# Linear attention feeding a tanh-shrink MLP: the kv product of batch 1 set between its transposes, the numerator beside the denominator, and batch 2's phi moved

## The chip, the cores and the metric

The kernel runs on one core of a Trainium2 chip. The metric is the device time of one execution in microseconds; the median of several runs is compared. PE is the matrix engine (TensorE), PEld its weight loads, DVE the vector engine, ACT the scalar engine, POOL GpSimd, and SP the engine whose queue issues most transfers.

## What is computed

q, k and v have 8 batches, 8 heads, 576 tokens and 64 features. Cut to what matters:

```python
def phi(x):
    return np.where(x > 0, x, np.exp(x) - 1.0) + 1.0
q_p, k_p = phi(q), phi(k)
kv  = einsum('bhsd,bhse->bhde', k_p, v)
z   = sum(k_p, axis=2)
num = einsum('bhsd,bhde->bhse', q_p, kv)
den = einsum('bhsd,bhd->bhs', q_p, z)[..., None] + 1e-06
x   = (num / den), heads joined: 4608 tokens x 512
h   = x @ w_in                  # 512 -> 2048
out = (h - tanh(h)) @ w_out     # 2048 -> 512
```

## The kernel before

**Two streams of work on one PE.** The MLP is cut into nine chunks of 512 tokens (the loop over `c`, with `NC = 9`). In each chunk the first layer (L366) has 16 steps `fi`, of four 128x512 matmuls each, and the second layer (L387) has 16 steps `s`, also of four. Between the steps the attention of a later batch is slipped in: the lists `s1[fi]` and `s2[s]` hold functions that are called after the matmuls of that step. In chunk `c` the attention of batch `n1 = c + 1` is finished, and phi of batch `n2 = c + 2` is computed. The order is written out by hand (`tc.manual_schedule()`): what the program says first stands first in its engine's queue, and only waits on semaphores are put in.

**PSUM banks.** There are eight. In chunk 0 the layer-1 steps go through all of them, and its layer 2 accumulates four output tiles in banks 0 to 3 at the same time: there `g = s // 4` is the group of four `fi` and `i = s % 4` the tile, so that steps 8 to 11 need the third quarter of `w_out` and steps 12 to 15 the last one. Attention work of chunk 0 goes through banks 4 to 7 in turn (`side`). From chunk 1 on the MLP uses banks 0 to 5 in turn (`dense`) and the attention banks 6 and 7 (`attn`).

**One batch of attention.** `phi_pieces` gives three instructions for half `i` of a batch: an exp on ACT (`e`, L134), max and add on DVE (`r`, L135) and a min on DVE (`y`, L136). qp is then transposed into `qT`, by PE and two copies (`a_qT_pe`: L164, copied out by ACT at L168 and by DVE at L170) for batch 1, and by a transposing transfer from SP's queue (`a_qT_dma`, L153) from batch 2 on. `a_kv` (L177, batch 1) and `a_kv_cols` (L199, later batches, on a widened copy of v, `vp`, L189) compute kv and z; a DVE multiplication with a mask puts them into `kz` (L186, L202). `a_den` makes the denominators (16 small matmuls at L276, then L281 and the reciprocal at L285). For batch 1 `a_split` cuts the reciprocals into two bf16 parts (L295 to L298, result `w`), `num1` computes the numerators (four small matmuls L320, four large L317) and ACT copies them into `ns` (L346, L344), and `spread1` spreads `w` over the partitions by matmuls (L354, eight for two pairs, banks 4 to 7) and multiplies (L359) into `xT`, the input of layer 1. For later batches the reciprocals go through DRAM (`a_spread`: L305, L308, tile `rdb`) and `a_num` multiplies the numerators with them (L317, L328). `b0_scale_rest` (L320, L263) is the last piece of batch 0.

**Work around the change.** ACT copies finished output tiles out of PSUM (`evac`, L396, tile `osb`), and SP stores them (L401). In layer 1, ACT computes tanh of two banks (L372) and DVE subtracts (`gT`, L373), which frees the banks. POOL issues the loads of q, k and v; `gate` (L383) is a copy on POOL that waits for qT, and the loads of the next batch stand behind it. q and k have one buffer each, so a load also waits until phi has read the batch before.

Of the kernel before, what the change touches and what calls it, by code (L numbers as in the profile page):

```python
# [18 lines left out]
def kernel(  # L19
# [43 lines left out]
    attn = Banks([6, 7])  # L63
# [78 lines left out]
    def a_kphi(b, i):  # L142
        phi(b, k_t, kp_t, "kp", i)
# [13 lines left out]
    def a_qT_pe(b, i, banks, on=None):  # L157
        if i == 0:
            new_qT(b)
        for n in range(2):  # L160
            j0, j1 = ((0, 5), (5, 9))[n]
            ps = banks().bitcast(BF16).rearrange("p (j t) -> p j t", t=128)
            for j in range(j0, j1):
                nc.tensor.transpose(ps[:, j - j0, :], qp_t[b][:, i, j].rearrange("p h d -> p (h d)"), ident)  # L164
            src = ps[:, 0:j1 - j0, :]
            dst = qT_t[b][:, i, j0:j1].rearrange("p j g t -> p j (g t)")
            if (on or "AV")[n] == "A":
                nc.scalar.copy(dst, src)  # L168
            else:
                nc.vector.tensor_copy(dst, src)  # L170
# [9 lines left out]
    def a_kv(b, banks):  # L180
        kz_t[b] = kz_c[b % 2]
        ps = [banks()[:, 0:384].rearrange("p (i e) -> p i e", i=2) for hg in range(2)]
        for i in range(2):
            kv_mm(b, i, [ps[hg][:, i, :] for hg in range(2)])
        for hg in range(2):
            nc.vector.tensor_mul(kz_t[b][:, hg], ps[hg][:, :, 0:160], mask[:, hg])  # L186
# [80 lines left out]
    def a_den(b, banks, parts=range(4)):  # L267

        kz, qT = kz_t[b], qT_t[b]
        ps = banks()[:, 0:J * 16]  # L270
        for t in range(4) if b == 0 else ():
            nc.tensor.matmul(ps[32 * t:32 * t + 32], eps[:, 0:32], one[:, 0:J * 16], start=True, stop=False)
        for n, p in enumerate((0, 2, 1, 3)):
            if n in parts:
                for t in range(4):
                    nc.tensor.matmul(ps[32 * t:32 * t + 32], kz[:, p // 2, p % 2, 128:160],  # L276
                                     qT[:, p % 2, :, p // 2, 16 * t:16 * t + 16],
                                     start=(n == 0 and b > 0), stop=(n == NP - 1))
        if b > 0:
            den = rpool.tile([128, J * 16], F32, name="den")  # L280
            nc.vector.tensor_scalar(den, ps, 1e-6, None, ALU.add)  # L281
        else:
            den = ps
        rden = rpool.tile([128, J * 16], F32, name="rden")
        nc.vector.reciprocal(rden, den)  # L285
        rden_t[b] = rden

    def a_split(b):

        f = rden_t[b]  # L290
        t1 = rpool.tile([128, J * 16], BF16, name="t1")
        u = rpool.tile([128, J * 16], F32, name="u")
        t2 = rpool.tile([128, J * 16], BF16, name="t2")
        w = rpool.tile([128, J * 16], BF16, name="w")
        nc.vector.tensor_copy(t1, f)  # L295
        nc.vector.scalar_tensor_tensor(u, t1, part[:, 0:1], f, ALU.mult, ALU.add)
        nc.vector.tensor_copy(t2, u)
        nc.vector.scalar_tensor_tensor(w, t2, part[:, 1:2], u, ALU.mult, ALU.add)  # L298
        rden_t[b] = w
# [202 lines left out]
    for c in range(NC):  # L502
        gT = gpool.tile([128, NF, 512], BF16, name="gT")
        n1, n2 = c + 1, c + 2
        s1 = {i: [] for i in range(16)}
        s2 = {i: [] for i in range(16)}
        if c == 0:
            side = Banks([4, 5, 6, 7])
            sub = {}

            def spread1(h):
                sub["bp"] = a_spread_pe(1, 4, (2 * h, 2 * h + 1))
                for p in (2 * h, 2 * h + 1):
                    a_scale(1, p, sub["ns"], sub["bp"], 144 * (p % 2))

            def num1():
                sub["ns"] = new_ns(1)
                for p in (NP, 0, 1, 2, 3):
                    a_num_copy(1, sub["ns"], p, side)

            s1[11].append(lambda: a_kphi(1, 0))
            s1[13].append(lambda: a_kphi(1, 1))
            s2[3].append(lambda: a_qphi(1, 0))
            s2[4].append(lambda: (a_qphi(1, 1), load_q(2), load_k(2), load_v(2)))
            s2[0].append(prepare)
            s2[7].append(lambda: (a_qT_pe(1, 0, side), a_qT_pe(1, 1, side), a_kv(1, side)))
            s2[8].append(lambda: b0_scale_rest(side))
            s2[9].append(lambda: a_den(1, side))
            s2[10].append(lambda: (num1(), a_split(1)))
            s2[11].append(lambda: spread1(0))  # L530

            def q2(n):
                if n == 0:
                    sub["q"] = [phi_pieces(2, q_t, qp_t, "qp", i) for i in range(2)]
                if n < 2:
                    for f in sub["q"][n][:2]:
                        f()
                else:
                    for x in sub["q"]:
                        x[2]()  # L540
                    a_qT_dma(2)

            s2[12].append(lambda: q2(0))
            s2[13].append(lambda: (spread1(1), q2(1)))
            s2[14].append(lambda: q2(2))
            s2[15].append(lambda: a_kphi(2, 0))
        elif n1 < B:
            s1[7 if c == 1 else 5].append(lambda: a_kv_cols(n1, attn))
            s1[10 if c == 1 else 8].append(lambda: (a_den(n1, attn), a_spread(n1)))
            for p in range(NP + 1):  # L550
                s2[(11 if c == 1 else 9) + p].append(lambda p=p: a_num(n1, p))
        if c == 1:
            s1[1].append(lambda: a_kphi(2, 1))
            for i in range(2):
                s1[3].append(lambda i=i: a_vp(2, i))
        if c >= 1 and n2 < B:

            s1[0].append(lambda: (gate(qT_t[n1]), load_k(n2), load_q(n2), load_v(n2)))
            d = 2
            s2[d].append(lambda: a_kphi(n2, 0))  # L560
            s2[d + 2].append(lambda: a_kphi(n2, 1))
            s2[d + 4].append(lambda: a_qphi(n2, 0))
            s2[d + 6].append(lambda: (a_qphi(n2, 1), a_qT_dma(n2)))
            for i in range(2):
                s2[14 + i].append(lambda i=i: a_vp(n2, i))
        if c == 0:

            first = Banks([4, 5, 6, 7, 0, 1, 2, 3])
            hs = [ps_all[:, n, :] for n in range(4)]
            order = [((0, 0), (0, 1)), ((2, 0), (2, 1), (0, 2), (0, 3), (2, 2), (2, 3)),  # L570
                     [(p, fi) for p in (1, 3) for fi in range(4)]]
            seen = [0] * 4
            for n, part_ in enumerate(order):
                if n == 1:
                    open2()
                for p, fi in part_:
                    l1mm(c, fi, hs[fi], p, seen[fi])
                    seen[fi] += 1
            for fi in range(4):
                l1act(fi, hs[fi], gT)  # L580
        for fi in range(4 if c == 0 else 0, NF):
            h = first() if c == 0 else dense()
            for p in range(NP):
                l1mm(c, fi, h, p, p)
            if c == 0:
                l1act(fi, h, gT)
            elif fi % 2:
                n = dense.order[(dense.n - 1) % 6]
                l1act2(fi - 1, ps_all[:, n - 1:n + 1, :], gT)
            for f in s1[fi]:  # L590
                f()
        os_ = {}
        for s in range(16):

            (g, i) = divmod(s, 4) if c == 0 else (s % 4, s // 4)
            if g == 0:
                os_[i] = ps_all[:, i, :] if c == 0 else dense()
            if c == NC - 1 and i == 3:

                if g == 0:  # L600
                    o2 = dense()
                    for o, f in ((os_[i], slice(0, 384)), (o2, slice(384, DM))):
                        for fi in range(NF):
                            nc.tensor.matmul(o[:, f], gT[:, fi, 384:512], w_out_sb[:, fi, f],
                                             start=(fi == 0), stop=(fi == NF - 1))
                        evac(c, i, o, f.start, f.stop)
                continue
            l2mm(gT, os_[i], i, 4 * g, 4 * g + 4)
            if g == 3:
                evac(c, i, os_[i])  # L610
            for f in s2[s]:
                f()
# [30 lines left out]
```

## Time and profile before

| what | value |
|---|---|
| median of 8 runs | 294.84 us (294.64 to 295.11) |
| the profiled execution's own time | 294.67 us |
| its span | 292.9 us |
| PE busy | 283.5 us, 97% of the span, 1772 instructions |
| DVE busy | 174.8 us, 60% |
| ACT busy | 139.6 us, 48% |
| granted TensorE clock | 0.999 |
| transfers | 38.94 MB in 39077 packets |

The span is that of the recorded instructions; the time of an execution is 1.8 us longer. Busy shares are means over the whole span. Chunk 0 with its layer 2 lies at about 17 to 51 us, chunk 1 at 51 to 82 us; after that a chunk takes about 30 us.

### The profile page before, as it was taken

The page shows a single profiled execution, that of the slowest core. Times are in us where ns is not written, and L with a number is a line of the kernel's source. Part 1 is how long each engine was busy: PE and PEld are TensorE (multiplying, and loading weights), DVE is VectorE, ACT ScalarE, POOL GpSimd, SP SyncE. Part 2 cuts the span into 40 slices and gives each one's busy share as a digit, 9 for nine tenths or more (in the row PEclk, how much of TensorE's full clock was granted, in tenths as well). Part 3 has the DMA queues.
Part 4 walks back from the last instruction along what each step waited for, and adds up shares of the span by engine and source line. Part 5 has one row for each costly group of instructions (what it writes and reads, how often), then busy time and mean ns, then how long its engine had stood idle before and what let it go on. Part 6 is the DMA issues. An engine that isn't in the chain of part 4 may idle for free.

```text
span 292.9 us, 4475 instructions
## 1 busy us (share of the span) xinstructions
PE 283.5 (97%) x1772; PEld 134.3 (46%) x1801; DVE 174.8 (60%) x265; ACT 139.6 (48%) x168; POOL 33.6 (11%) x55
## 2 busy tenths in 40 slices
PE   8999998999999999999999999999999999999994
PEld 2544453454444444544454445444444444444443
DVE  4759857887557764786478646865581457106600
ACT  4938537947344643465246524661552155126411
POOL 8673030030030003000300020000000000000000
PEclk9999999999999999999999999999999999999999
DMA  6999999998989658955895569666117310130032
GB/s 101 195 202 213 207 207 218 204 146 153 241 157 179 161 120 136 215 131 121 137 222 128 133 135 189 138 147 140 38 28 174 73 36 0 39 83 23 0 74 72
DMA packets 39077, 38.94 MB, mean 133 GB/s; under 512 B 16336, under 2 KB 33808, under 8 KB 38288
## 3 DMA queue, kind: packets, MB, share of 16 engines
q0 software_dynamic: 17552, 18.35, 38.6%
q1 hardware_dynamic: 21344, 20.17, 30.2%
q8 instruction: 14, 0.23, 0.3%
q10 hardware_dynamic: 160, 0.13, 0.1%
q14 instruction: 7, 0.06, 0.1%
HBM read 43.91 MB, written 9.55 MB: 183 GB/s over the span
## 4 chain that ended last, share of the span: by engine, by line
PE 75%; DMA 13%; issue 7%; POOL 2%; ACT 1%; DVE 0%; SPq 0%; POOLq 0%
PE ps_all L366 36%; PE ps_all L387 34%; DMA qraw<-in_q_dram 5%; DMA w_in_sb<-in_moe_w_in_dram 3%; PE ps_all L199 2%; DMA out_dram<-osb 2%; DMA kraw<-in_k_dram 2%; PE ps_all L317 2%; PE ps_all L276 1%; ACT osb L396 1%; SPq L401 0%; POOL qraw L90 0%; ACT e L134 0%; POOL kraw L93 0%; DVE qp L136 0%
## 5 line engine op out<-in xcount | busy, mean ns | idle before, releaser
L366 PE MATMUL ps_all<-xT,w_in_sb 128*128 128x512 bf16 x560 | 127.0, 379 | 1.1 <-DVE xT L244 0.3
L387 PE MATMUL ps_all<-w_out_sb,gT 128*128 128x512 bf16 x547 | 126.3, 379 | 0.7
L373 DVE TENSOR_TENSOR gT<-ps_all,th 128x1024 bf16<-128x1024 f32 x64 | 77.9, 1219 | 59.7 <-ACT th L372 59.7
L372 ACT ACTIVATE th<-ps_all 128x1024 f32<-128x1024 f32 x64 | 65.5, 1024 | 57.0 <-PE ps_all L366 46.4
L366 PEld LDWEIGHTS <-w_in_sb 128*128 128x128 bf16 x576 | 55.2, 98 | 66.6 <-issue 0.6
L387 PEld LDWEIGHTS <-gT 128*128 128x128 bf16 x560 | 54.1, 98 | 64.2 <-issue 0.2
L396 ACT COPY osb<-ps_all 128x512 f32<-128x512 f32 (+1 forms) x36 | 20.9, 583 | 73.4 <-PE ps_all L387 54.2
L328 DVE TENSOR_TENSOR xT<-ps_all,rdb 128x512 bf16<-128x512 f32 x24 | 16.4, 690 | 13.3 <-PE ps_all L317 11.2
L134 ACT ACTIVATE e<-qraw 128x1152 bf16<-128x1152 bf16 x16 | 18.5, 1162 | 6.9 <-DMA qraw<-in_q_dram 6.9
L134 ACT ACTIVATE e<-kraw 128x1152 bf16<-128x1152 bf16 x15 | 17.5, 1165 | 0.0
L136 DVE TENSOR_TENSOR qp<-e,r 128x1152 bf16<-128x1152 bf16 x16 | 12.0, 757 | 7.8 <-ACT e L134 7.2
L136 DVE TENSOR_TENSOR kp<-e,r 128x1152 bf16<-128x1152 bf16 x15 | 11.4, 758 | 8.1 <-ACT e L134 7.3
L383 POOL COPY g<-qT 1x1 bf16<-1x1 bf16 x5 | 1.4, 271 | 120.5 <-DMA qT<-qp 120.5
L378 DVE TENSOR_TENSOR gT<-ps_all,th 128x512 bf16<-128x512 f32 x16 | 10.3, 686 | 2.4 <-ACT th L377 1.7
L377 ACT ACTIVATE th<-ps_all 128x512 f32<-128x512 f32 x16 | 9.2, 598 | 4.3 <-PE ps_all L366 3.1
L317 PE MATMUL ps_all<-qT,kz 128*128 128x512 bf16 x28 | 10.1, 379 | 0.0
L444 PE MATMUL ps_all<-zero 128*128 128x512 bf16 x29 | 8.8, 463 | 1.2 <-DVE zero L405 1.2
L135 DVE TENSOR_SCALAR r<-qraw 128x1152 bf16<-128x1152 bf16 x16 | 7.3, 454 | 2.2 <-DMA qraw<-in_q_dram 2.2
L199 PE MATMUL ps_all<-vp,kp 64*128 64x136 bf16 x216 | 7.4, 220 | 0.4 <-POOL g L383 0.4
L199 PEld LDWEIGHTS <-kp 64*128 64x128 bf16 x216 | 6.4, 94 | 3.0 <-issue 2.1
L285 DVE RECIPROCAL rden<-den 128x144 f32<-128x144 f32 x7 | 7.4, 1053 | 0.2
L394 DVE COPY osb<-ps_all 128x128 f32<-128x128 f32 x1 | 0.3, 292 | 11.6 <-DMA out_dram<-osb 11.6
(82 smaller groups left out, 121.8 us busy)
## 6 DMA issues: line engine op xcount, KB each, us to landing
out_dram<-osb SPq DMA_DIRECT2D x70, 128.0 KB
rdb<-ds SPq DMA_DIRECT2D x12, 576.0 KB
kraw<-in_k_dram POOLq DMA_DIRECT2D x7, 576.0 KB, 7.1
qraw<-in_q_dram POOLq DMA_DIRECT2D x7, 576.0 KB, 9.3
v<-in_v_dram POOLq DMA_DIRECT2D x7, 576.0 KB, 11.7
w_out_sb<-in_moe_w_out_dram POOLq DMA_DIRECT2D x4, 512.0 KB, 16.1
w_in_sb<-in_moe_w_in_dram POOLq DMA_DIRECT2D x6, 256.0 KB, 9.0
qraw<-in_q_dram POOLq DMA_DIRECT2D x2, 288.0 KB, 4.5
```

Source lines behind the costliest of these rows:

```text
L134: return (lambda: nc.scalar.activation(e, x, AF.Exp), lambda: nc.vector.tensor_scalar(r, x, 0.0, 1.0, ALU.max, ALU.add), lambda: nc.vector ...
L136: lambda: nc.vector.tensor_tensor(y, e, r, ALU.min))
L199: nc.tensor.matmul(ps[hg][:, i, :], kp[r, i, j].rearrange("p h d -> p (h d)"), vp[r, i, j, :], start=(j == 0), stop=(j == J - 1))
L317: nc.tensor.matmul(ps, kz[:, p // 2, p % 2, 0:128], qT[:, p % 2, 0:8, p // 2, :], start=True, stop=True)
L328: nc.vector.tensor_mul(xT[:, p, S * b:S * b + 512].rearrange("p (j t c) -> p j t c", j=8, t=4), ps.rearrange("p j (t c) -> p j t c", t=4), ...
L366: nc.tensor.matmul(h, w_in_sb[:, 2 * (p % 2) + p // 2, fi * 128:(fi + 1) * 128], xT[:, p, c * 512:(c + 1) * 512], start=(n == 0), stop=(n ...
L372: nc.scalar.activation(th, h, AF.Tanh)
L373: nc.vector.tensor_sub(gT[:, fi:fi + 2, :], h, th)
L377: nc.scalar.activation(th, h, AF.Tanh)
L378: nc.vector.tensor_sub(gT[:, fi, :], h, th)
L387: nc.tensor.matmul(o, gT[:, fi, i * 128:(i + 1) * 128], w_out_sb[:, fi, :], start=(fi == 0), stop=(fi == NF - 1))
L396: nc.scalar.copy(osb[:, f0:f1], o[:, f0:f1])
```

## The change

It touches chunk 0's layer 2 and the start of chunk 1.

1. At step 7, `a_kv(1)` is called between the two halves of `a_qT_pe(1, ...)`, not behind both. The banks are handed out in that order, so the products go to banks 6 and 7, and the second half's transposes to 4 and 5 again.
2. `num1` and `a_split(1)` are called right behind `a_den(1)` at step 9, not at step 10: `num1` passes the four matmuls of step 10. The first spread stays behind step 11.
3. phi of batch 2: the exp of q's first half and its two DVE instructions move from step 12 to step 11, behind the first spread; on ACT this exp now stands ahead of the copy of the first output tile. The exp of the second half moves from step 13 to step 12 and that of k's first half from step 15 to step 13. On DVE the first min now stands ahead of the second spread's multiplications. SP's transposing transfer of batch 2's q moves from step 14 to step 13; in SP's queue it stood behind six output stores and now stands behind four.
4. `a_kv_cols(2)` in chunk 1 is called behind `fi = 8`, not `fi = 7`: its 36 matmuls move behind four of layer 1's. On DVE the order around it is the same as before.
5. The two calls of `a_vp(2, ...)` are written as one entry, in the same order.

```diff
-            s2[7].append(lambda: (a_qT_pe(1, 0, side), a_qT_pe(1, 1, side), a_kv(1, side)))
+            s2[7].append(lambda: (a_qT_pe(1, 0, side), a_kv(1, side), a_qT_pe(1, 1, side)))
             s2[8].append(lambda: b0_scale_rest(side))
-            s2[9].append(lambda: a_den(1, side))
-            s2[10].append(lambda: (num1(), a_split(1)))
+            s2[9].append(lambda: (a_den(1, side), num1(), a_split(1)))
             s2[11].append(lambda: spread1(0))
 
-            def q2(n):
-                if n == 0:
-                    sub["q"] = [phi_pieces(2, q_t, qp_t, "qp", i) for i in range(2)]
-                if n < 2:
-                    for f in sub["q"][n][:2]:
-                        f()
-                else:
-                    for x in sub["q"]:
-                        x[2]()
-                    a_qT_dma(2)
-
-            s2[12].append(lambda: q2(0))
-            s2[13].append(lambda: (spread1(1), q2(1)))
-            s2[14].append(lambda: q2(2))
-            s2[15].append(lambda: a_kphi(2, 0))
+            qs, ks = [], []
+
+            def exp2(pieces, src, store, name, i):
+                pieces.append(phi_pieces(2, src, store, name, i))
+                pieces[i][0]()
+
+            def rest2(f):
+                f[1]()
+                f[2]()
+
+            s2[11].append(lambda: (exp2(qs, q_t, qp_t, "qp", 0), rest2(qs[0])))
+            s2[12].append(lambda: exp2(qs, q_t, qp_t, "qp", 1))
+            s2[13].append(lambda: (spread1(1), exp2(ks, k_t, kp_t, "kp", 0), rest2(qs[1]), a_qT_dma(2)))
+            s2[14].append(lambda: rest2(ks[0]))
         elif n1 < B:
-            s1[7 if c == 1 else 5].append(lambda: a_kv_cols(n1, attn))
+            s1[8 if c == 1 else 5].append(lambda: a_kv_cols(n1, attn))
...
         if c == 1:
             s1[1].append(lambda: a_kphi(2, 1))
-            for i in range(2):
-                s1[3].append(lambda i=i: a_vp(2, i))
+            s1[3].append(lambda: (a_vp(2, 0), a_vp(2, 1)))
```

## The prediction, made before the changed kernel ran

> **What bounds the kernel now.** I read the page first, then the waits of PE, the timeline of 17 to 100 us, and the answers for single tiles.
>
> ```profile
> PE 283.5 (97%) x1772; PEld 134.3 (46%) x1801; DVE 174.8 (60%) x265; ACT 139.6 (48%) x168; POOL 33.6 (11%) x55
> PE ps_all L354 <- ACT ns L344: 0.7, 1, 0.7
> PE ps_all L199 <- POOL g L383: 0.4, 1, 0.4
> ```
>
> PE is the bound. The change leaves its matmuls as they are, so it can only win idle time of PE. The timeline (start, duration, engine, line; the idle time in brackets) shows three such gaps where the change works:
>
> ```profile
> 38.93 0.68 PE L164 MATMUL ps_all<-ident,qp 128*128 128x128 bf16 x9 [0.56 <-DVE qp L136]
> 39.54 1.66 PE L177 MATMUL ps_all<-v,kp 64*128 64x192 bf16 x36
> 41.13 1.04 PE L387 MATMUL ps_all<-w_out_sb,gT 128*128 128x512 bf16 x3
> 43.08 0.43 PE L276 MATMUL ps_all<-qT,kz 128*32 128x144 bf16 x16
> 44.31 0.28 PE L320 MATMUL ps_all<-qT,kz 128*128 128x64 bf16 x4
> 44.90 2.06 ACT L344 COPY ns<-ps_all 128x512 f32<-128x512 f32 x4
> 45.93 0.37 DVE L298 SCALAR_TENSOR_TENSOR w<-t,part,u 128x144 bf16<-128x144 bf16 x1
> 47.01 0.31 PE L354 MATMUL ps_all<-w,sel 32*128 32x144 bf16 x8 [0.69 <-ACT ns L344]
> 49.09 0.30 PE L354 MATMUL ps_all<-w,sel 32*128 32x144 bf16 x8
> ...
> 51.06 7.07 PE L366 MATMUL ps_all<-xT,w_in_sb 128*128 128x512 bf16 x31
> 53.23 2.62 SPq L153 DMA_TRANSPOSE qT<-qp  x1
> 56.85 1.22 DVE L373 TENSOR_TENSOR gT<-ps_all,th 128x1024 bf16<-128x1024 f32 x1
> 57.99 0.82 DVE L189 COPY vp<-v 128x1152 bf16<-128x1152 bf16 x2
> 58.50 1.24 PE L199 MATMUL ps_all<-vp,kp 64*128 64x136 bf16 x36 [0.37 <-POOL g L383]
> 62.36 0.43 PE L276 MATMUL ps_all<-qT,kz 128*32 128x144 bf16 x16
> 78.68 2.00 DVE L328 TENSOR_TENSOR xT<-ps_all,rdb 128x512 bf16<-128x512 f32 x3 [2.08 <-DMA rdb<-ds]
> ```
>
> Matmuls overlap, so I count from start to start: four MLP matmuls take 0.87 us (0.216 each), a transposed half 0.61, kv 1.59, den 0.36. The gaps: 0.62 before 38.93; 47.01 where PE could have gone on at 46.17; and 32 matmuls from 51.06 end their turn at 57.97, kv starts at 58.50. (POOL's copy is only named because it ended last; kv's first weights wait for `vp`, which ends near 58.4.) Three landings matter. They are the answers for the tiles v, w_out_sb and qraw, in windows that hold one load each, issued at 22.50, 23.23 and 38.54; the figure counts from the issue:
>
> ```profile
> DMA to landing us min/median/max: 16.0/16.0/16.0
> DMA to landing us min/median/max: 17.8/17.8/17.8
> DMA to landing us min/median/max: 7.9/7.9/7.9
> ```
>
> **kv between the transposes.** qp's second half is ready at 38.87 and its banks 4 and 5 are empty at 39.21, so kv covers the 0.62. But kv needs v of batch 1, landed at 22.50 + 16.0 = 38.50: it starts at 38.55, not 38.31, the second half at 40.14, and PE is through at 40.75, against 41.13. Step 8 is the first to use the third quarter of w_out, landed at 23.23 + 17.8 = 41.03. So step 8 starts at 41.08: gain 0.05, and 0.3 goes into a new wait. Nothing the change moves is issued before these loads, so I keep their times.
>
> The Trainium skill, "DMA: Bandwidth & Descriptors", section "Anatomy of one DMA — SWDGE (gpsimd) path", fits such a transfer as about 2 us plus bytes over 436 GB/s; 512 KB would take an estimated 3.2 us. By that w_out would be no gate and the gain would be 0.33 larger. The measured 17.8 us under load decides.
>
> **num beside den.** den starts at 41.08 + 1.95 (43.08 - 41.13) = 43.03, the numerators at 43.39 instead of 44.31. Three things must be done before the spread. ACT's copies end 2.65 behind the start of L320 (44.31 to 46.96): 46.04. `w` ends 3.22 behind den's start (43.08 to 46.30): 46.25. PE: 0.12 + 0.87 for the numerators, 1.84 for eight MLP matmuls (47.25 to 49.09): 46.22. Inside `num1`, the third large matmul waits until DVE has read den's bank (about 43.82, needed at 43.94), the fourth for ACT's first copy, as before. So `w` is last, and the spread starts at 46.36 against 47.01: cumulative gain 0.65, with only 0.14 of the gap left.
>
> **phi of batch 2.** On ACT, exp(q0) now stands before the copy of output tile 0. q(2) lands at 38.54 + 7.9 = 46.44. ACT is free at 46.04, so exp runs 46.47 to 47.62; the tile is complete at 47.63, so the copy loses nothing. By starts in the trace (1.06 from an exp to the copy behind it, 0.47 from a copy to an exp) follow exp(q1) 48.10, copy 49.16, exp(k0) 49.63 (k landed at 39.27 + 10.2 = 49.47), copies 50.7 and 51.2, tanh 52.3. Layer 1 of chunk 1 needs banks 1 and 2 at 51.27 and 52.14; they are free at 49.75 and 51.3. On DVE, r and min of q0 (1.3 us) stand between the two scale pairs: first pair 46.79 to 48.21, min done 49.43, second pair to 50.77. Layer 1 starts at 46.36 + 2.08 + 1.97 = 50.41, and its third and fourth matmul need that pair at 50.84 and 51.06; ready at 50.06 and 50.77. Cost: nothing, with 0.3 to spare.
>
> The Trainium skill, "TensorE: Matmul & The Clock Gate", section "Architectural detail: the array is 16× 32×32, not 1× 128×128", calls the queues of ACT and DVE strict FIFO. That speaks against this edit: a late q holds the output copies too, at the price under (d), where a queue that could reorder would lose nothing. With the landing of the trace both give the same sum.
>
> **kv of batch 2 behind fi = 8.** DVE sets this stage: tanh at 52.3 starts gT(0,1) at 53.4 (before: 54.48), min of k1 follows, gT(2,3) ends at 57.0, `vp` at 57.4 and 57.8. Step 8 takes bank 2, free at 57.0, at 50.41 + 6.91 = 57.32; kv comes at 58.2 + 0.1 for the change of tile shape (0.1 is what the same step costs at 87.12, with 24 matmuls in 5.28). The 0.53 shrinks to 0.1: 0.43 more. den of batch 2 comes at 58.29 + 1.17 + 1.73 + 0.1 = 61.29 against 62.36: 1.07 in all. Its `kz` now has two steps between, not three: DVE is through at 60.7.
>
> **Does it last?** The next tight place is 78.68: DVE waits for `rdb`, and the third numerator (79.58) takes the bank that the first multiplication empties at 79.37: 0.2 to spare. `rdb` goes back to the transposing transfer (gates the loads of batch 3, which fill the transfers until 70.4, when `ds` lands too). The transfer waits for q1's min at about 52.0 instead of SP's stores until 53.23: 1.2 earlier, against 1.07 for PE. It lasts. Two stores move behind the transfer and share with it; they may eat this margin. From there on chunks are paced by PE, and a gain is carried to the end.
>
> **Sum.** 0.05 + 0.60 + 0.42 = 1.07. The profiled span becomes 291.8 us, its execution 294.67 - 1.07 = 293.6; with the median 0.17 above it, 293.8.
>
> **Rivals.** (a) w_out and v land earlier in other executions or in the changed one: the first gap is won too, up to 0.38 more: 293.4. Against it: the loads before are the same. (b) The `rdb` chain does not move: the third numerator waits until 79.4 instead of 78.5 and about 0.9 is given back: 294.7; halfway 294.2. For it: the spare 0.2, the two stores. (c) The DVE chain does not start earlier (tanh or the mins late): bank 2 comes free at 58.07, step 8 stalls 0.8, and kv's move wins nothing: 294.6. (d) Slower: q(2) lands late and exp(q0) holds ACT. Tile 2's copy ends 4.9 behind the landing and is needed at 52.14, so a landing after 47.3 costs PE one for one; from 48.3 the gain is gone. The loads of q land after 9.3 us in the median (47.8, price 0.6); if it landed with k at 49.5, the price were 2.2: 296.0. Against it: the 7.9 measured, and an unchanged issue.
>
> **Chances.** The forecast 0.58, (a) 0.14, (b) 0.12, (c) 0.08, (d) 0.08. About 0.2% (0.6 us) can be told from no change: faster takes the forecast, (a) and a third of (b), 0.76; (c) and the rest of (b) are the same, 0.16; slower 0.08. The forecast's own range is 293.5 to 294.2 (landings off by some 0.3). The range reaches to (a) and a little below, and to (b) and (c): 293.2 to 294.7.
>
> **What would show it.** Right: PE L387 near 41.1 behind a wait for w_out; L354 at 46.4, released by `w`; layer 1 at 50.4; kv at 58.3 behind 36 matmuls without a wait; den at 61.3; L328 at 77 to 77.6. Wrong: ACT idle before exp(q0) longer than 0.5; PE waiting for the copies L396 at 51 to 52.5, for gT before 57.5, or for xT L328 at 78.5.

## The result, and the profile after

The changed kernel takes 293.77 us (median of 10 runs, 293.36 to 293.95) against 294.84 us: a ratio of 0.996, 95% interval 0.9952 to 0.9968. That is 1.07 us faster, and 293.8 us had been forecast.

The profiled execution took 293.92 us with a span of 292.1 us. From the page, the busy time of the engines:

```profile
PE 283.1 (97%) x1772; PEld 134.1 (46%) x1801; DVE 175.0 (60%) x265; ACT 139.6 (48%) x168; POOL 33.3 (11%) x55
```

PE does the same work as before; what went is idle time. From the waits of PE in the same run, the line that is new:

```profile
PE ps_all L387 <- DMA w_out_sb<-in_moe_w_out_dram: 0.2, 1, 0.2
```

And its timeline (start us, duration us, engine, line, operation; in brackets the idle time in front and what ended it):

```profile
38.98 1.66 PE L177 MATMUL ps_all<-v,kp 64*128 64x192 bf16 x36
40.57 0.68 PE L164 MATMUL ps_all<-ident,qp 128*128 128x128 bf16 x9
41.48 1.02 PE L387 MATMUL ps_all<-w_out_sb,gT 128*128 128x512 bf16 x3 [0.24 <-DMA w_out_sb<-in_moe_w_out_dram]
43.42 0.43 PE L276 MATMUL ps_all<-qT,kz 128*32 128x144 bf16 x16
44.38 2.06 ACT L344 COPY ns<-ps_all 128x512 f32<-128x512 f32 x4
46.27 0.37 DVE L298 SCALAR_TENSOR_TENSOR w<-t,part,u 128x144 bf16<-128x144 bf16 x1
46.70 0.30 PE L354 MATMUL ps_all<-w,sel 32*128 32x144 bf16 x8
47.45 1.16 ACT L134 ACTIVATE e<-qraw 128x1152 bf16<-128x1152 bf16 x1 [1.01 <-DMA qraw<-in_q_dram]
...
50.74 7.93 PE L366 MATMUL ps_all<-xT,w_in_sb 128*128 128x512 bf16 x35
58.61 1.24 PE L199 MATMUL ps_all<-vp,kp 64*128 64x136 bf16 x36
61.61 0.43 PE L276 MATMUL ps_all<-qT,kz 128*32 128x144 bf16 x16
77.90 2.03 DVE L328 TENSOR_TENSOR xT<-ps_all,rdb 128x512 bf16<-128x512 f32 x3 [2.05 <-DMA rdb<-ds]
```

Read against the lines of before: kv (L177) runs between the transposes, and step 8 (L387 at 41.48) now waits for `w_out`. The spread (L354) follows `w`, which ends at 46.64, not the copies. In chunk 1, 36 matmuls run without a break up to kv (L199); the trace holds records of 35 of them, from 50.74 on, and no wait.

**How two profiles are laid side by side.** In this execution the loads of the start came later: the third quarter of `w_out` was issued at 23.61, not 23.23. Every time here is therefore some 0.35 us later than the prediction's, and the two profiled executions differ by 0.75 us, not by 1.07. So the experiments below are compared by intervals between events of one profile, in us:

| kernel | w_out landed to den of batch 1 | den of batch 1 to den of batch 2 | den of batch 2 to chunk 2 | third numerator behind the second | chunk 2 to the end |
|---|---|---|---|---|---|
| before | 2.05 | 19.28 | 19.49 | 1.08 | 211.05 |
| changed | 2.01 | 18.19 | 19.49 | 1.08 | 211.05 |
| kv of batch 1 alone | 1.96 | 19.29 | 19.91 | 1.50 | 211.01 |
| num alone | 1.99 | 18.64 | 19.56 | 1.16 | 211.07 |
| phi alone | 2.04 | 18.85 | 19.63 | 1.22 | 211.04 |
| kv of batch 2 alone | 2.03 | 19.01 | 19.90 | 1.49 | 211.01 |
| changed, kv of batch 1 put back | 2.02 | 18.19 | 19.52 | 1.12 | 211.04 |
| changed, kv of batch 2 put back | 2.02 | 18.20 | 19.64 | 1.24 | 211.04 |
| changed, no wait for w_out | 1.53 | 18.19 | 19.74 | 1.34 | 211.04 |
| before, no wait for w_out | 2.02 | 19.29 | 19.49 | 1.08 | 211.05 |
| changed, q late | 1.94 | 20.61 | 19.49 | 1.08 | 211.03 |

The events are the landing of the third quarter of `w_out` (its issue plus its time to landing, which is given to 0.1 us), the first matmuls of L276 for batches 1 and 2, the first L366 of chunk 2, and the second and third L317 of chunk 1. The change took 1.09 us out of the second column and nothing beyond 0.04 us out of the others. The first column is the same in nearly every kernel, but for two reasons. With kv between the transposes, step 8 waits for that landing. With the old order, PE waits for the second half of `qp` of batch 1, and the chain to it starts with an exp that waits for its own load. In the kernel before:

```profile
35.69 2.22 ACT L134 ACTIVATE e<-qraw 128x1152 bf16<-128x1152 bf16 x2 [3.42 <-DMA qraw<-in_q_dram]
```

In all eight profiles with the old order this exp starts 5.34 to 5.40 us ahead of the landing of `w_out`, and den comes 7.39 or 7.40 us behind the exp. So the two limits lie within the precision of each other, and the first column alone can't tell them apart; experiment 3 does. What lies behind chunk 2's start is the same to 0.08 us in every profile.

### The profile page after: what moved, and what is told of

Same layout as the page of the kernel before. It is cut to its first block, busy times and chain, and to the rows that moved or that the text cites. A ratio compares the mean times of both kernels' runs of the same rounds, so it can differ in the third digit from the quotient of the medians.

```text
span 292.1 us, 4470 instructions
## 1 busy us (share of the span) xinstructions
PE 283.1 (97%) x1772; PEld 134.1 (46%) x1801; DVE 175.0 (60%) x265; ACT 139.6 (48%) x168; POOL 33.3 (11%) x55
## 4 chain that ended last, share of the span: by engine, by line
PE 80%; DMA 14%; POOL 2%; issue 1%; ACT 1%; SPq 0%; DVE 0%; POOLq 0%
PE ps_all L366 38%; PE ps_all L387 37%; DMA w_out_sb<-in_moe_w_out_dram 6%; DMA w_in_sb<-in_moe_w_in_dram 3%; DMA out_dram<-osb 2%; PE ps_all L199 2%; DMA kraw<-in_k_dram 2%; PE ps_all L317 2%; PE ps_all L276 1%; POOL v L419 1%; ACT osb L396 1%; SPq L401 0%; POOL qraw L90 0%; PE ps_all L320 0%; POOL w_out_sb L115 0%
## 5 line engine op out<-in xcount | busy, mean ns | idle before, releaser
L366 PE MATMUL ps_all<-xT,w_in_sb 128*128 128x512 bf16 x560 | 127.0, 379 | 1.1 <-DVE xT L244 0.3
L387 PE MATMUL ps_all<-w_out_sb,gT 128*128 128x512 bf16 x547 | 126.1, 379 | 0.9 <-DMA w_out_sb<-in_moe_w_out_dram 0.2
L366 PEld LDWEIGHTS <-w_in_sb 128*128 128x128 bf16 x576 | 55.3, 98 | 66.6 <-issue 0.6
L387 PEld LDWEIGHTS <-gT 128*128 128x128 bf16 x560 | 54.2, 98 | 64.5 <-issue 0.4
L134 ACT ACTIVATE e<-qraw 128x1152 bf16<-128x1152 bf16 x16 | 18.5, 1160 | 8.4 <-DMA qraw<-in_q_dram 8.4
L317 PE MATMUL ps_all<-qT,kz 128*128 128x512 bf16 x28 | 10.1, 379 | 0.0
L199 PEld LDWEIGHTS <-kp 64*128 64x128 bf16 x216 | 6.4, 94 | 2.5 <-issue 2.5
L199 PE MATMUL ps_all<-vp,kp 64*128 64x136 bf16 x216 | 7.4, 220 | 0.0
```

The lines of the kernel that those rows point to most:

```text
L134: return (lambda: nc.scalar.activation(e, x, AF.Exp), lambda: nc.vector.tensor_scalar(r, x, 0.0, 1.0, ALU.max, ALU.add), lambda: nc.vector ...
L199: nc.tensor.matmul(ps[hg][:, i, :], kp[r, i, j].rearrange("p h d -> p (h d)"), vp[r, i, j, :], start=(j == 0), stop=(j == J - 1))
L317: nc.tensor.matmul(ps, kz[:, p // 2, p % 2, 0:128], qT[:, p % 2, 0:8, p // 2, :], start=True, stop=True)
L366: nc.tensor.matmul(h, w_in_sb[:, 2 * (p % 2) + p // 2, fi * 128:(fi + 1) * 128], xT[:, p, c * 512:(c + 1) * 512], start=(n == 0), stop=(n ...
L387: nc.tensor.matmul(o, gT[:, fi, i * 128:(i + 1) * 128], w_out_sb[:, fi, :], start=(fi == 0), stop=(fi == NF - 1))
```

## The experiments

All were timed against the kernel before on the same chip; a ratio stands with its 95% interval. Kernels of different groups ran on different chips, so their times are not compared closer than some 0.2 us.

**1. Only kv of batch 1 between the transposes.**

```diff
-            s2[7].append(lambda: (a_qT_pe(1, 0, side), a_qT_pe(1, 1, side), a_kv(1, side)))
+            s2[7].append(lambda: (a_qT_pe(1, 0, side), a_kv(1, side), a_qT_pe(1, 1, side)))
```

> Only kv of batch 1 moved between its transposes. By my theory the wait for qp goes, but the third quarter of w_out (landing 17.8 us after its issue) takes its place: 294.8 us, a gain of 0.05 or less, and PE waits for w_out at step 8 by about 0.3 us. Rival (the first gap is won, 0.38): 294.4 us.

Measured: 294.92 us against 294.91, ratio 1.0003 (0.9993 to 1.0013). Its timeline shows both landings that took the gap's place:

```profile
39.18 1.66 PE L177 MATMUL ps_all<-v,kp 64*128 64x192 bf16 x36 [0.23 <-DMA v<-in_v_dram]
41.70 1.02 PE L387 MATMUL ps_all<-w_out_sb,gT 128*128 128x512 bf16 x3 [0.25 <-DMA w_out_sb<-in_moe_w_out_dram]
```

The wait for qp became a wait for v and one for `w_out`. From there on the first two columns are as before, but for 0.09 us within the precision of the landing (0.1). The theory stands. The profiled execution was the slowest of the eleven (295.61 us): it lost 0.42 us at the third numerator, with nothing moved ahead of it.

**2. The changed kernel with that edit undone** (the diff above, reversed).

> The changed kernel with kv of batch 1 put back behind both transposes. Theory: w_out gates step 8 at the same moment, so nothing is lost: 293.8 us (up to 0.05 more). Rival (the first gap was won by the change): 294.1 to 294.4 us.

Measured: 293.74 us against 294.92, ratio 0.9957 (0.9943 to 0.997). The whole gain is there without the move of kv, and the first two columns agree to 0.01 us with those of the changed kernel.

**3. Without the wait for w_out.** Chunk 0's steps 8 to 11 take the rows of the second quarter, which landed long before. The output is then another one; the work and the loads are the same:

```diff
-            l2mm(gT, os_[i], i, 4 * g, 4 * g + 4)
+            l2mm(gT, os_[i], i, 4 * g, 4 * g + 4, 4 if c == 0 and g == 2 else 0)
...
-            nc.tensor.matmul(o, gT[:, fi, i * 128:(i + 1) * 128], w_out_sb[:, fi, :],
+            nc.tensor.matmul(o, gT[:, fi, i * 128:(i + 1) * 128], w_out_sb[:, fi - shift, :],
```

On the changed kernel:

> The changed kernel with steps 8 to 11 of chunk 0 reading the second quarter of w_out instead of the third (a changed computation with the same work and the same loads): the wait for the landing is gone. Theory: 0.2 to 0.35 us less than the changed kernel, 293.45 to 293.6 us. Rival (w, the copies or q's landing are late next and eat it): 293.8 us.

On the kernel before:

> The kernel before with the same replacement in steps 8 to 11 (third quarter of w_out not read in chunk 0). Theory: there PE came to step 8 only when w_out had landed, so nothing changes: 294.8 us. Rival (w_out held the kernel before too): 294.5 us.

Measured: 293.61 us against 294.92 for the changed kernel, ratio 0.9954 (0.9941 to 0.9966), and 295.0 us, ratio 1.0001 (0.9992 to 1.001), for the one before. The wait is gone in the first and nothing moves in the second, as expected. The first time lies at the slow end of what was expected: in its profile den of batch 1 comes 0.48 us sooner against the landing, but the third numerator stands 1.34 us behind the second, not 1.08, so 0.26 us was given back there, and 0.22 stay. Between 293.61 and experiment 2's 293.74 on the same chip the times alone decide nothing; that the gate is `w_out` rests on the profiles. In that of the changed kernel without the wait:

```profile
35.73 2.22 ACT L134 ACTIVATE e<-qraw 128x1152 bf16<-128x1152 bf16 x2 [3.18 <-DMA qraw<-in_q_dram]
42.70 0.43 PE L276 MATMUL ps_all<-qT,kz 128*32 128x144 bf16 x16
```

From the exp of batch 1's q to den (L276) it takes 6.97 us here and 7.39 in the second kernel, both without the wait; with it, 7.38 in the changed kernel and 7.40 in experiment 2. So the move of kv is worth 0.42 us where `w_out` does not gate step 8, and 0.02 where it does.

**4. Only num beside den.**

```diff
-            s2[9].append(lambda: a_den(1, side))
-            s2[10].append(lambda: (num1(), a_split(1)))
+            s2[9].append(lambda: (a_den(1, side), num1(), a_split(1)))
```

> Only num1 and a_split moved beside den. Theory: the wait of 0.7 us before the first spread shrinks to about 0.15, and everything behind is paced by PE, so 0.6 is kept: 294.25 us. Rival (w and the copies end no earlier, or DVE and ACT behind are not paced by PE): 294.6 to 294.8 us.

Measured: 294.14 us against 294.91, ratio 0.9978 (0.9969 to 0.9987). The second column falls by 0.64 us. This is the larger half of the change.

**5. Only phi of batch 2 moved** (the block from `s2[11]` to `s2[15]` of the diff).

> Only phi of batch 2 moved. Theory: tanh of the first two steps of chunk 1 comes 0.4 us earlier on ACT (the exp of k is out of its way), the chain gT, vp ends near 58.0 instead of 58.4 us, and the gap of 0.5 us before kv of batch 2 nearly closes: 294.4 us. Rival (phi alone moves nothing on PE's path, the gap is closed by moving kv): 294.8 us; rival (exp waits for q and holds the output copies): 295 us or more.

Measured: 294.71 us against 294.91, ratio 0.9995 (0.9986 to 1.0004): not told from no change, and a miss by the time, for which 294.4 had been expected. In the profile the mechanism was there: tanh of the first two steps starts at 53.02 (before: 53.41), `vp` begins at 57.58 instead of 57.99, and kv starts with no wait:

```profile
58.09 1.24 PE L199 MATMUL ps_all<-vp,kp 64*128 64x136 bf16 x36
```

The second column falls by 0.43 us, and 0.14 us came back at the third numerator. But the profiled execution took 294.40 us and is one of four of the eleven that lie between 294.33 and 294.40; the other seven took 294.69 to 295.02. What those lost, and where, no profile shows.

**6. Only kv of batch 2 behind fi = 8.**

```diff
-            s1[7 if c == 1 else 5].append(lambda: a_kv_cols(n1, attn))
+            s1[8 if c == 1 else 5].append(lambda: a_kv_cols(n1, attn))
```

> Only kv of batch 2 moved behind fi = 8. Theory: the step in front of it then waits about 0.16 us for bank 2 (gT(2,3) ends at 58.07, needed at 57.97), and kv waits no more: a gain of 0.25, 294.6 us. If the parts were additive, the four alone would sum to 1.07; by the theory they sum to 1.3, since phi and this one work on the same gap.

Measured: 294.86 us against 294.91, ratio 1.0002 (0.9993 to 1.001). A miss: no time, although the second column falls by 0.27 us. The timeline of chunk 1's end shows where it went:

```profile
79.34 1.89 DVE L328 TENSOR_TENSOR xT<-ps_all,rdb 128x512 bf16<-128x512 f32 x3 [2.64 <-DMA rdb<-ds]
79.46 0.10 PEld L317 LDWEIGHTS <-kz 128*128 128x128 bf16 x1
80.09 0.38 PE L317 MATMUL ps_all<-qT,kz 128*128 128x512 bf16 x1 [0.25 <-DVE xT L328]
```

`rdb` lands at 79.3, the first multiplication empties its bank at 80.03, and the third numerator, whose weights were loaded at 79.46, waits until 80.09: 0.4 us late. Two things add up there. Den comes 0.27 us sooner, while POOL's copy that stands ahead of the loads of batch 3, and with it the chain to `rdb`, begins where it had (17.00 us behind the landing of `w_out`, 17.01 before). And from the start of that copy to the multiplication by `rdb` it took 20.92 us, 20.64 in the profile of the kernel before, with 0.15 to 0.2 us to spare there. So about half of the loss is what had been won at kv, given back because the landing did not move with it, and half is scatter of the landing: experiment 1's profile lost as much with nothing won ahead of it.

**7. The same with the third numerator called later,** and its control, the kernel before with that edit alone:

```diff
-                s2[(11 if c == 1 else 9) + p].append(lambda p=p: a_num(n1, p))
+                s2[(11, 12, 14, 14, 15)[p] if c == 1 else 9 + p].append(lambda p=p: a_num(n1, p))
```

> kv of batch 2 behind fi = 8 alone, with the same later third numerator. kv alone gave no time, although den of batch 2 came 0.28 us earlier behind step 8: the third numerator then waited 0.4 us for the multiplication by rdb. Theory: with that wait out of the way the 0.25 us appear: 294.4 to 294.6 us, den of batch 2 21.0 us behind step 8 (before: 21.23), and no wait at the third numerator. Rival (the move itself is worth nothing): 294.85 us, as the control.

> The kernel before, with one thing added: in chunk 1 the third numerator is called behind step 14 together with the fourth, not behind step 13, so that it can wait 0.87 us longer for the bank that the first multiplication (and rdb) empties. Control for the next kernel. Theory (rdb lands with a scatter of some 0.3 us and takes back what is won ahead of it): 294.6 to 294.85 us, and 0.1 at most is won, since the spare was 0.2 us; the gap between the second and third numerator shows no wait. Rival (rdb never cost anything): 294.9 us.

Measured: 294.55 us against 294.94, ratio 0.9985 (0.9976 to 0.9994), with kv moved; 294.84 us, ratio 0.9993 (0.9984 to 1.0001), for the control. In the two profiles the distance from den to chunk 2 is 19.49 and 19.48 us, with no wait at the numerators, and den of batch 2 comes 19.00 us behind that of batch 1 with kv moved and 19.29 without: 0.29 us, and 0.29 between the medians. The two intervals overlap, but on this one chip ten of the eleven runs with kv moved took 294.61 us or less, and ten of the eleven of the control 294.66 or more. The size rests on the profiles, and there the theory stands: kv's move is worth 0.29 us by itself, where `rdb` does not take it back.

**8. The changed kernel with kv of batch 2 put back behind fi = 7** (experiment 6's diff, reversed).

> The changed kernel with kv of batch 2 put back behind fi = 7 (parts 1 to 3 alone). Theory: once phi has been moved, vp ends near 57.4 when PE comes to kv at 57.4: the move is worth 0.05 us or less, 293.8 us, and the wait of PE before kv is under 0.1. Rival (the move closes the gap, 0.4): 294.1 to 294.2 us.

Measured: 293.92 us against 294.94, ratio 0.9969 (0.9956 to 0.9981). The second column is 18.20, that of the changed kernel to 0.01 us, and kv, behind fi = 7, starts with no wait:

```profile
57.31 1.24 PE L199 MATMUL ps_all<-vp,kp 64*128 64x136 bf16 x36
```

Once phi has been moved, `vp` is ready when PE comes to kv, and moving kv adds nothing. The median is 0.15 us above the changed kernel's, on another chip and from five runs between 293.64 and 294.56; the profile is of the fastest, and 0.16 us was lost at the third numerator even there. The other pairing, phi left out and the rest kept, was not tried.

**9. q of batch 2 late.**

```diff
-            ... load_q(2), load_k(2), load_v(2)))
+            ... load_k(2), load_q(2), load_v(2)))
```

> The changed kernel with the loads of batch 2 issued in the order k, q, v: q lands where k did, near 49.5 us. By the price under rival (d), the copy of tile 2 ends 4.9 us behind the landing and PE waits for its bank 2.2 us: 296.0 us, slower than before. Rival (exp can be late without cost, ACT has slack or the queue goes on): 293.8 us.

Measured: 296.12 us against 294.92, ratio 1.0038 (1.0025 to 1.0051): slower than before, by the price of rival (d). From its timeline:

```profile
49.93 1.16 ACT L134 ACTIVATE e<-qraw 128x1152 bf16<-128x1152 bf16 x1 [3.68 <-DMA qraw<-in_q_dram]
51.62 0.59 PE L366 MATMUL ps_all<-xT,w_in_sb 128*128 128x512 bf16 x2 [0.91 <-ACT osb L396]
52.60 0.38 PE L366 MATMUL ps_all<-xT,w_in_sb 128*128 128x512 bf16 x1 [0.39 <-DVE xT L359]
53.27 1.24 PE L366 MATMUL ps_all<-xT,w_in_sb 128*128 128x512 bf16 x5 [0.29 <-DVE xT L359]
54.06 1.07 ACT L396 COPY osb<-ps_all 128x512 f32<-128x512 f32 x2
54.70 6.20 PE L366 MATMUL ps_all<-xT,w_in_sb 128*128 128x512 bf16 x27 [0.19 <-ACT osb L396]
```

ACT stood still for 3.68 us with a finished output tile behind the exp in its queue, and PE paid first for tile 0's bank, then, behind the min on DVE, for the scaled `xT`, and last, after the eight matmuls of the first two steps, for tile 2's bank. q landed 11.1 us behind its issue, at 49.8; the copy of tile 2, the first of the two at 54.06, ended at 54.64. The second column grows by 2.42 us over the changed kernel's.

**10. A version meant to beat both:** the changed kernel with `b0_scale_rest` in front of step 8, den and num one step earlier, and the later third numerator.

```diff
-            s2[7].append(lambda: (a_qT_pe(1, 0, side), a_kv(1, side), a_qT_pe(1, 1, side)))
-            s2[8].append(lambda: b0_scale_rest(side))
-            s2[9].append(lambda: (a_den(1, side), num1(), a_split(1)))
+            s2[7].append(lambda: (a_qT_pe(1, 0, side), a_kv(1, side), a_qT_pe(1, 1, side), b0_scale_rest(side)))
+            s2[8].append(lambda: (a_den(1, side), num1(), a_split(1)))
...
-                s2[(11 if c == 1 else 9) + p].append(lambda p=p: a_num(n1, p))
+                s2[(11, 12, 14, 14, 15)[p] if c == 1 else 9 + p].append(lambda p=p: a_num(n1, p))
```

> A version meant to beat both: the changed kernel with the last piece of batch 0 (b0_scale_rest) ahead of step 8, where PE waits for w_out anyway, with den, num1 and a_split of batch 1 one step earlier (step 8), and with the later third numerator of chunk 1. Theory: 0.12 us of matmuls go into the wait for w_out, and w and the copies are ready before PE comes to the spread, so its 0.14 us go too: 293.5 us, the first spread near 46.1 with no wait. Rival (w_out lands later than PE needs it anyway, or exp waiting for q and rdb eat it): 293.75 us.

Measured: 293.55 us against 294.94, ratio 0.9953 (0.9941 to 0.9965). From its timeline:

```profile
40.98 0.28 PE L320 MATMUL ps_all<-qT,kz 128*128 128x64 bf16 x4
41.26 1.02 PE L387 MATMUL ps_all<-w_out_sb,gT 128*128 128x512 bf16 x4
45.08 0.37 DVE L298 SCALAR_TENSOR_TENSOR w<-t,part,u 128x144 bf16<-128x144 bf16 x1
46.26 0.30 PE L354 MATMUL ps_all<-w,sel 32*128 32x144 bf16 x8
```

The small matmuls fill the wait for `w_out`, and `w` is ready 0.8 us before the spread, which waits for nothing. Den of batch 2 comes 20.00 us behind the landing of `w_out` (changed kernel: 20.20), and 19.48 us lie from there to chunk 2. Against the kernel before this is faster; against the changed kernel the 0.2 us lies inside the intervals, so that it beats that too is likely from the profile and not shown by the times.

## Why the prediction was right, point by point

- **kv of batch 1, forecast 0.05.** Step 8 started at 41.48, with `w_out` issued at 23.61 and landed 17.8 us later: 0.07 us behind the landing. Experiments 1, 2 and 3 show that this edit is worth nothing here and why: without the wait for `w_out` it would be worth 0.42 us (0.38 by the prediction). In the profiles this load landed 17.7 to 18.5 us behind its issue, with others in flight. By the fit of the Trainium skill, "DMA: Bandwidth & Descriptors", section "Anatomy of one DMA — SWDGE (gpsimd) path", it would have landed after an estimated 3.2 us; that did not hold for this load.
- **num beside den, forecast 0.60.** 0.64 us in experiment 4. `w` was last, as forecast, and the copies (done at 46.44) just ahead of it.
- **phi of batch 2, forecast to cost nothing.** True, but with less to spare than written. q landed 8.5 us behind its issue, not 7.9, and exp began at 47.45; moved by the 0.35 us that this execution was late, 46.8 had been expected. ACT stood idle for 1.01 us in front of it, and more than 0.5 had been named as a sign of being wrong. That sign was set too tight: by the prediction's own price under (d) a landing costs nothing up to 47.3, which is 1.26 us of idle time behind 46.04. Tile 2's copy ended near 52.2 (51.58 and 0.58 us), needed at 50.74 + 1.73 = 52.47: 0.3 us to spare, where the prediction's figures had 0.8. Rival (d) was real: experiment 9 gave 296.12 us for the 296.0 worked out from a landing at 49.5. The place was right: PE waited for tile 0's bank and for `xT` on the way, but the wait that ended last was the one for tile 2's bank, whose copy ended 4.8 us behind the landing (4.9 forecast).
- **kv of batch 2, forecast 0.43.** Size right, cause misplaced: the prediction priced the earlier DVE chain under the move of kv, and it is phi's move that makes the chain earlier. Phi alone takes 0.43 us out of the second column, kv alone 0.27 us, and kv on top of phi nothing. They close the same gap. The sum came out because the change has both.
- **Does it last, forecast yes with 0.2 us to spare.** In the profiled run it did: the third numerator stands 1.08 us behind the second, as before. The chain to `rdb` moved as forecast: POOL's copy comes 15.73 us behind the landing of `w_out`, 17.01 before, so 1.28 us sooner (forecast 1.2). But the margin is thinner than the scatter of the landing behind it, so that nothing at all came back is luck in part. Where it fell short, up to 0.42 us came back at the third numerator. Rival (b) is a part of single executions and not a case apart; the prediction's 0.58 for the plain forecast was rather high for that.
- **Sum.** 1.07 forecast; 0.04 + 1.09 us between events of the two profiles, 1.07 us between the medians. That the median fell within 0.03 us of the 293.8 forecast is luck: the changed kernel's own runs lie between 293.36 and 293.95.

## What to carry to other kernels

An idle gap in front of a landing is won only up to that landing: before filling one, list what the program needs next and when each of it arrives. Two edits that close the same gap do not add up, and one that gains nothing alone may have been taken back by the next gate; intervals between events of one profile show both, where medians only show zero. When an instruction that waits for a transfer is moved ahead of one that does not on an in-order engine, price the landing's lateness, since everything behind it is held too.

## What the runs showed that had not been expected

The fourteen profiles differ by more than 0.08 us ahead of chunk 2 only: from its start to the end it took 210.99 to 211.07 us, whatever had been changed. The landing of `rdb` scatters more than the gains in dispute: from the start of POOL's copy ahead of the loads of batch 3 to the start of the first multiplication by `rdb` 20.64 to 21.23 us passed, with much the same transfers each time; why it scatters was not settled.
